# A hand-ordered attention and MoE kernel: one chunk's convolution moves from TensorE to VectorE, and the written order of all work is replaced

## The chip, the cores and the metric

The kernel runs on one core of a Trainium2 chip. The metric is the device time of one execution in microseconds (us). Three runs of the kernel before gave 212.16, 212.40 and 213.29 us, median 212.4.

## The reference

Two stages follow each other. The first is a gated linear attention with a running state of 48x48 for each of 4 batches and 8 heads over 768 steps. The second takes its output x (768 steps of 384 channels for each batch), makes a gate by a causal convolution over 5 steps, and multiplies the gate with a projection:

```python
f = 1 / (1 + exp(-f_logit))
for t in range(768):
    state = f[t][:, None] * state + outer(k[t], v[t])
    y[t] = q[t] @ state
x = y, heads side by side                      # 4 x 768 x 384
gate_pre[t] = sum(conv_w[j] * x[t - 4 + j] for j in range(5))   # channel by channel
out = (sigmoid(gate_pre) * (x @ w_val)) @ w_out
```

Everything is float32. The weights of the second stage come as int64 pairs (float64 bits) and are turned into float32 on the chip.

## The kernel before

**Chunks and units.** The 768 steps are cut into 6 chunks of 128 (C = 128, chunk c). A pair of heads lies on 112 of the 128 partitions, and BP = 16 is 4 batches x 4 pairs. The second stage goes in 8 units: chunk 0 is units 0 and 1 (two batches each), chunks 1 to 4 are units 2 to 5 (four batches each), chunk 5 is units 6 and 7 (two batches each).

**Attention in a chunk.** ScalarE makes exp and ln of the gate logits (`pexp`, `pln`, tile `e`), VectorE sums the logarithms along the steps (`scan`), ScalarE makes the two exponentials (`exp2`, `exp1`), VectorE multiplies them into k and q (`pmulk`, `pmulq`, tiles `kb`, `qb`). For each batch b, TensorE then makes the scores of 8 heads (`scores`, into the one PSUM tile `aps`), VectorE masks them while it copies them to SBUF (`mask`, tile `asb`), and TensorE applies them to v and adds q times the old state (`apply`, into a PSUM bank `bk`). ScalarE copies the result into `xf` (`xevac`). In parallel TensorE transposes k (`ktrans`), ScalarE copies it (`kevac`, tile `ksb`), TensorE makes the state's increment (`dstate`), and VectorE adds and decays it (`stadd`, `stmul`); a DMA (`stcopy`) puts the new state in place.

**Second stage of a unit.** `msplit` (ScalarE) and `mlow` (VectorE) split x into two parts, `mval` is its projection on TensorE (9 matmuls for each of 3 column blocks m), `mmul` (VectorE) multiplies it by the gate, `mhigh` (ScalarE) and `mrest` (VectorE) split the product, `mout` (TensorE, 9 matmuls) projects it out, and `mstore` (ScalarE) copies it to one of two buffers `osb`, from which a DMA stores it. The gate itself has two forms. Either TensorE convolves (`conv n j`, five taps j, 12 matmuls of 32x32 blocks each, every float32 matmul two instructions in the trace; tile `wd` holds the taps), and `gate` (ScalarE) takes the sigmoid from PSUM. Or ScalarE makes the last tap (`mlast n m`) and VectorE adds the other four, one `SCALAR_TENSOR_TENSOR` each (`mtap n m j`, gt <- xf, cws, gt), before `gate`. Before, units 0 to 3 (chunks 0 to 2) use TensorE, units 4 to 7 VectorE. The constant CS = 3 is the first chunk whose channels are laid out for the second form: `place`, `wturn` and `halo` turn by it, and in chunk CS the 4 steps of the chunk before (`halo`) come by DMAs (tile `xf`), in other chunks by a VectorE copy.

**What sets the order.** Nothing is scheduled by a tool: the string PROGRAM lists every piece of work, and `Ordered` chains each engine's instructions (TensorE, VectorE, ScalarE, and SyncE, which issues all DMAs) in just that order. An engine takes its list one by one; a piece that waits for another engine holds up all behind it on its own engine. Between engines there are only data dependencies: `aps` is one tile, so the next `scores` waits for the `mask` before it, and the six banks `bk` are handed round.

`busy n` puts n bfloat16 matmuls on a tile of zeros (tile `idle`) on TensorE; their result is not used.

```python
def busy(n):
    for _ in range(n):
        PE.matmul(free[-1][:], idle[:, 0:128], idle[:], start=True, stop=True)
```

All the operations are emitted through one helper line, so that the profile names them all L119 and tells them apart by their tiles. The kernel ends with a check of ranges (`okc`, `sums`, `cnt`), on whose result a general path, not taken here, would run.

Of the kernel before, what the change touches and what calls it, by code (L numbers as in the profile page):

```python
# [32 lines left out]
CS = 3  # L33
# [11 lines left out]
halo 0; loadf 0 0; loadf 0 1; loadv 0 1; wload 0; loadk 0 1; loadv 0 2; loadv 0 0; loadq 0 0; loadq 0 1; pexp 0 0;  # L45
loadk 0 0; loadk 0 2; loadq 0 2; loadf 1 0; pln 0 0; pexp 0 1; wload 1; scan 0 0; weight 0; wload 2; pln 0 1;
loadk 1 0; exp2 0 0; scan 0 1; exp1 0 0; loadv 1 0; pexp 0 2; loadf 2 0; pmulq 0 0; exp2 0 1; loadq 1 0; exp1 0 1;
pmulk 0 1; pln 0 2; pmulk 0 0; busy 24; ktrans 0 1; pmulq 0 1; ktrans 0 0; kevac 0 1; scores 0 0; scan 0 2;
kevac 0 0; weight 0; dstate 0 0; dstate 0 1; weight 0; exp2 0 2; weight 0; weight 0; mask 0 0; exp1 0 2;
pmulk 0 2; busy 4; scores 0 1; pexp 1 0; apply 0 0; loadk 2 0; pmulq 0 2; ktrans 0 3; okc 0; xevac 0 0; ktrans 0 2;  # L50
mask 0 1; weight 1; pln 1 0; scores 0 3; stadd 0 0; weight 0; stcopy 0 0; taps; weight 2; kevac 0 2; apply 0 1;
kevac 0 3; scan 1 0; weight 2; dstate 0 3; loadv 2 0; dstate 0 2; xevac 0 1; loadq 2 0; weight 1; conv 0 0;
conv 0 1; msplit 0; weight 2; conv 0 2; exp2 1 0; weight 2; conv 0 3; weight 2; conv 0 4; exp1 1 0; mask 0 3;
gate 0 1; scores 0 2; pmulk 1 0; apply 0 3; stadd 0 1; gate 0 2; loadk 2 1; gate 0 0; mask 0 2; loadf 3 0;
ktrans 1 0; xevac 0 3; ktrans 1 1; kevac 1 0; weight 2; apply 0 2; kevac 1 1; scan 1 1; weight 2; dstate 1 1;
loadv 2 1; dstate 1 0; xevac 0 2; weight 2; msplit 1; conv 1 0; loadq 2 1; conv 1 1; weight 4; pexp 2 0;
stadd 1 0; conv 1 2; stcopy 0 1; pmulq 1 0; conv 1 3; conv 1 4; weight 1; scores 1 1; weight 1; weight 1;
exp2 1 1; mask 1 1; gate 1 2; pmulk 1 1; scores 1 0; gate 1 1; apply 1 1; loadk 3 0; mask 1 0; exp1 1 1; halo 1;
ktrans 1 3; weight 1; ktrans 1 2; mlow 0; apply 1 0; xevac 1 1; kevac 1 2; pmulq 1 1; weight 1; dstate 1 2;
kevac 1 3; weight 1; wturn 0; stmul 1 0; scores 1 2; xevac 1 0; okc 1; pln 2 0; mlow 1; weight 3; mval 0 0;  # L60
stcopy 1 0; mask 1 2; mval 1 1; loadv 3 0; weight 3; loadq 3 0; scan 2 0; wturn 1; weight 4; apply 1 2; pexp 3 0;
mval 1 2; mmul 1 1; weight 3; xevac 1 2; mval 0 2; weight 3; exp2 2 0; weight 3; dstate 1 3; exp1 2 0;
mmul 1 2; scores 1 3; mmul 0 2; weight 3; pln 3 0; mval 0 1; loadk 3 1; mask 1 3; mval 1 0; pmulq 2 0; weight 3;
apply 1 3; gate 1 0; weight 3; mmul 0 1; weight 4; weight 4; xevac 1 3; loadv 3 1; loadq 3 1; weight 4;
msplit 2; conv 2 0; halo 2; weight 4; conv 2 1; mmul 0 0; weight 4; conv 2 2; mmul 1 0; weight 4; pmulk 2 0;
conv 2 3; mhigh 0 0; mlow 2; scores 2 1; mhigh 1 2; mhigh 0 2; mhigh 0 1; ktrans 2 0; mhigh 1 1; conv 2 4; mrest 0 2;
kevac 2 0; mrest 0 0; mhigh 1 0; mrest 0 1; dstate 2 0; mrest 1 1; mout 0 1; mrest 1 2; gate 2 1; mrest 1 0;
gate 2 2; mout 0 2; mask 2 1; gate 2 0; mstore 0 1; mval 2 1; stadd 1 1; mstore 0 2; stmul 1 1; scan 2 1; loadf 4 0;
stcopy 1 1; scores 2 0; mout 0 0; mmul 2 1; exp2 2 1; mask 2 0; mout 1 0; mout 1 2; scan 3 1; mstore 0 0; mstore 1 0;
apply 2 0; exp1 2 1; pexp 4 0; pmulk 2 1; apply 2 1; okc 2; pmulq 2 1; ktrans 2 3; loadq 4 0; xevac 2 0; ktrans 2 2;  # L70
xevac 2 1; scan 3 0; ktrans 2 1; scores 2 2; kevac 2 2; loadk 4 0; kevac 2 1; kevac 2 3; dstate 2 2; dstate 2 1;
exp2 3 1; dstate 2 3; mask 2 2; loadv 4 0; mval 2 2; exp1 3 1; stadd 2 1; mstore 1 2; pmulq 3 1; pln 4 0; scores 2 3;
mmul 2 2; apply 2 2; pmulk 3 1; loadk 4 1; exp2 3 0; stadd 2 0; exp1 3 0; ktrans 3 3; stmul 2 0; ktrans 3 2;
pmulk 3 0; xevac 2 2; stcopy 2 0; mout 1 1; kevac 3 2; kevac 3 3; dstate 3 2; pmulq 3 0; mstore 1 1; ktrans 3 1;
ktrans 3 0; mhigh 2 1; dstate 3 3; mask 2 3; kevac 3 1; mval 2 0; kevac 3 0; mhigh 2 2; mrest 2 1; mrest 2 2;
scores 3 1; mmul 2 0; dstate 3 1; okc 3; mhigh 2 0; stmul 2 1; dstate 3 0; mrest 2 0; apply 2 3; loadf 5 0;
stadd 3 0; stmul 3 0; mout 2 0; scan 4 1; xevac 2 3; loadq 4 1; loadv 4 1; msplit 3; halo 3; conv 3 0; mstore 2 0;
mlow 3; stcopy 2 1; exp2 4 1; conv 3 1; exp1 4 1; conv 3 2; mask 3 1; conv 3 3; pexp 5 0; pmulk 4 1; scores 3 0;
pmulq 4 1; conv 3 4; pln 5 0; loadk 5 0; mask 3 0; apply 3 1; stadd 3 1; gate 3 0; stmul 3 1; apply 3 0; scan 5 0;
xevac 3 1; scores 3 2; gate 3 2; loadv 5 0; stcopy 3 0; xevac 3 0; ktrans 4 2; scan 5 1; gate 3 1; mval 3 0;  # L80
loadq 5 0; kevac 4 2; mask 3 2; exp2 5 1; dstate 4 2; mval 3 2; mmul 3 0; scan 4 0; exp1 5 1; scores 3 3; apply 3 2;
loadk 5 1; mmul 3 2; exp2 4 0; mask 3 3; mout 2 2; exp1 4 0; pmulk 4 0; xevac 3 2; okc 4; exp2 5 0; apply 3 3;
pmulq 4 0; mstore 2 2; pmulk 5 1; exp1 5 0; scores 4 0; stcopy 3 1; pmulk 5 0; xevac 3 3; ktrans 4 0; mout 2 1;
loadv 5 1; kevac 4 0; loadq 5 1; pmulq 5 0; mask 4 0; mval 3 1; mhigh 3 2; mhigh 3 0; mrest 3 2; mstore 2 1;
mrest 3 0; apply 4 0; mlast 4 2; mmul 3 1; mlast 4 0; mtap 4 2 0; mhigh 3 1; scores 4 1; mtap 4 0 0; xevac 4 0;
mrest 3 1; msplit 4; ktrans 4 1; mask 4 1; mout 3 1; kevac 4 1; mtap 4 0 1; mlast 4 1; mtap 4 0 2; dstate 4 1;
mstore 3 1; mout 3 0; mtap 4 2 1; mtap 4 2 2; mlow 4; scores 4 3; mstore 3 0; apply 4 1; halo 4; mtap 4 1 0;
mtap 4 1 1; ktrans 4 3; xevac 4 1; mask 4 3; mval 4 1; kevac 4 3; mtap 4 1 2; mtap 4 2 3; apply 4 3; okc 5; gate 4 2;
pmulq 5 1; scores 4 2; mtap 4 1 3; xevac 4 3; mtap 4 0 3; dstate 4 3; gate 4 1; dstate 4 0; mask 4 2; mout 3 2;
gate 4 0; stadd 4 0; mmul 4 1; apply 4 2; mstore 3 2; stmul 4 0; stadd 4 1; mhigh 4 1; stcopy 4 0; stmul 4 1;  # L90
scores 5 1; xevac 4 2; mrest 4 1; stcopy 4 1; halo 5; mlast 5 1; mval 4 0; mask 5 1; mtap 5 1 0; scores 5 0;
mtap 5 1 1; mmul 4 0; apply 5 1; mask 5 0; mhigh 4 0; mrest 4 0; apply 5 0; xevac 5 1; mtap 5 1 2; mlast 5 0;
# [38 lines left out]
def gla_moe(ctx: ExitStack, tc: tile.TileContext, q, k, f, v, wv, cw, wo, out):  # L131
# [165 lines left out]
    slot = lambda c, b: (B * c + b) % 2  # L297
    place = lambda c, m, z: (z + TURN[m]) % 4 if c >= CS else z

# [419 lines left out]
```

## Time and profile before

| what | before |
|---|---|
| median of 3 runs | 212.4 us |
| the profiled execution | 211.6 us, of which its span is 209.9 us |
| TensorE matmuls busy | 190.1 us |
| TensorE weight loads busy | 151.8 us |
| VectorE busy | 171.5 us |
| ScalarE busy | 133.3 us |
| GpSimd busy | 17.9 us |
| mean granted TensorE clock | 0.98 |

The profile shows one execution. Its engines are PE (TensorE matmuls), PEld (TensorE weight loads), DVE (VectorE), ACT (ScalarE), POOL (GpSimd) and SP (SyncE). Busy time is the union of an engine's instructions. A row of groups gives the engine, the operation, output <- input, the number of instructions, their busy time in us, the mean of one in ns, and the idle time just ahead of them with what ended it. A row of windows gives from:to, the length, the busy time of each engine with its instructions, the granted clock, the DMA engines' share and GB/s. A row of waits reads: who waited, for whom, us in total, times, the longest. A row of the timeline or of the chain begins with the start in us and the length.

### The profile page before, as it was taken

The numbers are of one execution on the slowest core, as the hardware profiler recorded it, in microseconds if no ns is written. First come the engines' busy times: TensorE is split into PE (matmuls) and PEld (weight loads), VectorE is DVE, ScalarE is ACT, GpSimd is POOL, SyncE is SP. The second block draws the span as 40 slices with busy tenths as digits, with TensorE's granted clock in tenths as the row PEclk, the third lists the DMA queues.
The fourth block names the chain that finished last, engine by engine and source line by source line (L and its number), as shares of the span: only waits on it lengthen the run. The fifth ranks groups of instructions, "written<-read, shape, count | busy, mean of one in ns | idle before, by whom it ended". The sixth has DMA issues, their size and how long they took to land.

```text
span 209.9 us, 6753 instructions
## 1 busy us (share of the span) xinstructions
PE 190.1 (91%) x2974; PEld 151.8 (72%) x2974; DVE 171.5 (82%) x233; ACT 133.3 (63%) x205; POOL 17.9 (9%) x19
## 2 busy tenths in 40 slices
PE   0988959869998989999999999999999999999970
PEld 0356748658995579988857788788888888798970
DVE  6469987867989989899799999698979999797700
ACT  3677974976995665796299866663642843744630
POOL 4000200603120910000000000000000000000000
PEclk9999997979999999999999999999999999999998
DMA  5899999963595037464395633702022001200431
GB/s 181 262 419 430 411 418 334 403 210 100 127 292 203 31 80 250 141 204 130 119 292 164 170 123 105 242 2 104 3 65 46 3 0 50 103 0 3 150 125 41
DMA packets 20372, 34.28 MB, mean 163 GB/s; under 512 B 10992, under 2 KB 13296, under 8 KB 19184
## 3 DMA queue, kind: packets, MB, share of 16 engines
q1 hardware_dynamic: 20336, 33.78, 47.7%
q8 instruction: 25, 0.41, 0.9%
q14 instruction: 11, 0.09, 0.1%
HBM read 26.77 MB, written 4.72 MB: 150 GB/s over the span
## 4 chain that ended last, share of the span: by engine, by line
PE 73%; DVE 10%; DMA 5%; issue 3%; POOL 3%; SPq 2%; ACT 1%; ACTq 0%; DVEq 0%
PE bk L119 61%; PE aps L119 11%; DMA qb<-in_q 3%; POOL woL L254 3%; DVE e L119 2%; DVE qb L119 2%; DVE asb L119 2%; SPq L119 2%; DMA out<-osb 2%; DVE cb L119 1%; DVE ca L119 1%; DVE kb L119 1%; ACT osb L119 1%; ACT woH L119 0%; DVE ss L119 0%
## 5 line engine op out<-in xcount | busy, mean ns | idle before, releaser
L119 ACT ACTIVATE e<-e 112x1024 f32<-112x1024 f32 (+2 forms) x42 | 48.7, 1177 | 7.5 <-DMA e<-in_f 4.1
L119 DVE TENSOR_TENSOR asb<-aps,tri 128x1024 f32<-128x1024 f32 x24 | 29.4, 1223 | 10.0 <-PE aps L119 9.0
L119 PE MATMUL bk<-asb,vb 128*32 128x128 f32 x768 | 36.1, 283 | 0.0
L119 PE MATMUL aps<-qb,kb 48*128 48x128 f32 x384 | 29.7, 292 | 5.8 <-DVE asb L119 3.9
L119 PEld LDWEIGHTS aps<-qb,kb 48*128 48x128 f32 x384 | 24.5, 192 | 13.6 <-issue 5.5
L119 PEld LDWEIGHTS bk<-asb,vb 128*32 128x32 f32 x768 | 31.3, 114 | 0.8 <-issue 0.2
L119 PE MATMUL bk<-qb,st 112*32 112x128 f32 x480 | 30.6, 281 | 0.0
L119 PE MATMUL bk<-rg,woH 128*128 128x512 f32 (+1 forms) x108 | 29.9, 363 | 0.0
L119 DVE TENSOR_TENSOR_SCAN e<-keep,e 112x1024 f32<-112x1024 bf16 (+1 forms) x13 | 27.5, 2119 | 2.8 <-ACT e L119 2.8
L119 ACT COPY osb<-bk 128x256 f32<-128x256 f32 (+1 forms) x24 | 11.5, 479 | 21.7 <-PE bk L119 14.6
L119 PEld LDWEIGHTS bk<-qb,st 112*32 112x32 f32 x480 | 21.8, 112 | 4.4 <-issue 2.6
L119 ACT COPY xf<-bk 128x384 f32<-128x384 f32 x24 | 11.5, 478 | 17.8 <-PE bk L119 17.7
L119 PEld LDWEIGHTS bk<-rg,woH 128*128 128x128 f32 x108 | 18.4, 188 | 3.0 <-issue 0.4
L119 PE MATMUL bk<-rg,woL 128*128 128x512 f32 (+1 forms) x54 | 19.3, 357 | 0.9 <-POOL woL L254 0.9
L119 DVE SCALAR_TENSOR_TENSOR gt<-xf,cws,gt 128x512 f32<-128x512 f32 x24 | 17.5, 747 | 0.3
L119 DVE TENSOR_TENSOR qb<-qb,e 112x1024 f32<-112x1024 f32 (+1 forms) x13 | 16.1, 1236 | 1.9 <-DMA qb<-in_q 1.9
L119 PE MATMUL bk<-xf,wd 32*32 32x256 f32 (+1 forms) x480 | 16.4, 487 | 0.9 <-ACT xf L119 0.6
L119 PE MATMUL bk<-xH,wvH 128*128 128x512 f32 (+1 forms) x42 | 15.6, 372 | 0.0
L119 ACT CAST rg<-gt 128x512 fp32r<-128x512 f32 (+1 forms) x18 | 9.4, 547 | 8.9 <-DVE gt L119 7.1
L119 DVE TENSOR_TENSOR kb<-kb,e 112x1024 f32<-112x1024 f32 (+1 forms) x13 | 14.7, 1138 | 0.2 <-DMA kb<-in_k 0.2
L119 PE MATMUL bk<-xL,wvH 128*128 128x512 f32 (+1 forms) x42 | 14.5, 344 | 0.0
L119 PE MATMUL bk<-xH,wvL 128*128 128x512 f32 (+1 forms) x42 | 14.5, 344 | 0.0
(90 smaller groups left out, 313.1 us busy)
## 6 DMA issues: line engine op xcount, KB each, us to landing
e<-in_f SPq DMA_DIRECT2D x5, 1024.0 KB, 8.8
kb<-in_k SPq DMA_DIRECT2D x9, 512.0 KB, 4.5
qb<-in_q SPq DMA_DIRECT2D x9, 512.0 KB, 5.5
vb<-in_v SPq DMA_DIRECT2D x9, 448.0 KB, 5.1
out<-osb SPq DMA_DIRECT2D x12, 256.0 KB, 2.0
out<-osb SPq DMA_DIRECT2D x12, 128.0 KB, 1.7
st<-ss SPq DMA_DIRECT2D x20, 72.0 KB, 2.6
raww<-in_wv SPq DMA_DIRECT2D x1, 1152.0 KB, 10.4
```

The lines of the kernel that those rows point to most:

```text
L119: ins = emit(*a, **kw)
L254: nc.gpsimd.tensor_tensor(out=dst[1], in0=x, in1=dst[0].bitcast(F32), op=ALU.subtract)
```

## The change

CS goes from 3 to 2. In PROGRAM the five `conv 3 j` are gone (unit 3 is chunk 2), and three `mlast 3 m` and twelve `mtap 3 m j` are there instead. The whole string is written in a new order. The fillers were `busy 24` and `busy 4` and are `busy 20`, `busy 3`, `busy 2` and `busy 5`. No function is changed.

```diff
-CS = 3
+CS = 2
...
-pmulk 0 1; pln 0 2; pmulk 0 0; busy 24; ktrans 0 1; pmulq 0 1; ktrans 0 0; kevac 0 1; scores 0 0; scan 0 2;
...
+scan 0 1; loadv 1 0; exp2 0 0; loadq 1 0; exp1 0 0; pmulk 0 0; pln 0 2; pmulq 0 0; busy 20; ktrans 0 0; scores 0 0;
...
```

The order at three places, as the built kernels have it. The number behind a tile's name is its address slot, so `asb_83` and `asb_84` are the two buffers of masked scores; x4 behind a row counts equal instructions that follow one another; L119 is L120 in the changed kernel.

VectorE, at the start of the real work, before (two scans of chunk 0, then q, k, k, q of its first two pieces, the third scan, the first mask):

```order
L119 SCALAR_TENSOR_TENSOR e_79<-keep,e_79 112x512 x2
L119 TENSOR_TENSOR qb_64<-qb_64,e_79 112x512
L119 TENSOR_TENSOR kb_66<-kb_66,e_82 112x512 x2
L119 TENSOR_TENSOR qb_64<-qb_64,e_79 112x512
L119 SCALAR_TENSOR_TENSOR e_79<-keep,e_79 112x1024
```

VectorE at the same place now:

```order
L120 SCALAR_TENSOR_TENSOR e_79<-keep,e_79 112x512 x2
L120 TENSOR_TENSOR kb_66<-kb_66,e_82 112x512
L120 TENSOR_TENSOR qb_64<-qb_64,e_79 112x512
L120 SCALAR_TENSOR_TENSOR e_79<-keep,e_79 112x1024
L120 TENSOR_TENSOR qb_64<-qb_64,e_79 112x512
L120 TENSOR_TENSOR kb_66<-kb_66,e_82 112x512
```

The first piece's k and q stand first now, and the large scan comes between the two pieces. In the queue of loads, which SyncE issues, the first pieces of k and q have moved ahead of those of v and of the small weight `cw`.

TensorE in chunk 0, before (two transposes, the third scores, an apply, two state increments, and the first convolution matmul of unit 0):

```order
L119 MATMUL bk_111<-ident,kb_66 128x112 x4
L119 MATMUL bk_112<-ident,kb_66 128x112 x4
L119 MATMUL aps<-qb_64,kb_66 128x128 x8
L119 MATMUL bk_107<-asb_84,vb_68 32x128 x16
L119 MATMUL bk_108<-vb_68,ksb_88 48x48 x8
L119 MATMUL bk_108<-vb_68,ksb_87 48x48 x8
L119 MATMUL bk_110<-xf_91,wd 32x256
```

TensorE at the same place now:

```order
L120 MATMUL bk_111<-ident,kb_66 128x112 x4
L120 MATMUL bk_112<-ident,kb_66 128x112 x4
L120 MATMUL aps<-qb_64,kb_66 128x128 x8
L120 MATMUL bk_107<-vb_68,ksb_88 48x48 x8
L120 MATMUL bk_109<-asb_84,vb_68 32x128 x16
L120 MATMUL bk_107<-vb_68,ksb_87 48x48 x8
L120 LDWEIGHTS idle
L120 MATMUL bk_109<-idle 128x512
```

An increment stands ahead of the apply, and fillers stand where the convolution of unit 0 stood; that convolution comes after the fourth scores and their apply.

VectorE around the first mask of chunk 3, before (a state product, the next scan, the low part of unit 3's x, the mask, k and q of chunk 4, the next mask):

```order
L119 TENSOR_TENSOR ss<-u_89,e_79 112x384
L119 SCALAR_TENSOR_TENSOR e_80<-keep,e_80 112x1024
L119 TENSOR_TENSOR xL<-xf_91,xH 128x1536
L119 TENSOR_TENSOR asb_84<-aps,tri 128x1024
L119 TENSOR_TENSOR kb_66<-kb_66,e_82 112x1024
L119 TENSOR_TENSOR qb_64<-qb_64,e_80 112x1024
L119 TENSOR_TENSOR asb_83<-aps,tri 128x1024
```

VectorE there now, from the first mask of chunk 3 on:

```order
L120 TENSOR_TENSOR asb_84<-aps,tri 128x1024
L120 SCALAR_TENSOR_TENSOR gt<-xf_91,cws,gt 128x512 x4
L120 TENSOR_TENSOR u_90<-ss,bk_110 112x384
L120 TENSOR_TENSOR gt<-bk_107,gt 128x512
L120 TENSOR_TENSOR asb_83<-aps,tri 128x1024
L120 TENSOR_TENSOR xL<-xf_91,xH 128x1536
L120 TENSOR_TENSOR rg_907<-gt,rg_906 128x512
L120 SCALAR_TENSOR_TENSOR gt<-xf_91,cws,gt 128x512 x3
L120 TENSOR_TENSOR asb_83<-aps,tri 128x1024
```

The twelve taps of unit 3 stand here in runs of four, three and five between the masks (the five lie some rows further down, and hold the last tap of one block and the four of the next).

More of the change, by code (lines that the diff above doesn't have):

```diff
@@ L50 @@
[L50 to L89, printed above, removed]
@@ L106 @@
+mstore 6 0; mrest 7 2; gate 7 1; mmul 7 1; mhigh 7 1; mout 5 2; mstore 5 0; mrest 7 1; mout 7 1; mstore 5 2;
+mout 7 2; mstore 7 1; mout 7 0; mstore 7 2; mout 6 2; mstore 7 0; mstore 6 2
 """
```

79 lines of the change are left out of this document (59 added, 20 removed).

## The prediction

> **What bounds the kernel now.** I began with the page: the span, the engines' busy time, and its slices.
>
> ```profile
> span 209.9 us, 6753 instructions
> PE 190.1 (91%) x2974; PEld 151.8 (72%) x2974; DVE 171.5 (82%) x233; ACT 133.3 (63%) x205; POOL 17.9 (9%) x19
> PE   0988959869998989999999999999999999999970
> DVE  6469987867989989899799999698979999797700
> PEclk9999997979999999999999999999999999999998
> ```
>
> TensorE is near full from the second slice on, and without a hole over the last two thirds. VectorE is next, at nine tenths for most of the way. The averages hide where the kernel still has room, so I cut the span: the front (up to chunk 2's first scores, about 69 us), the body up to the last VectorE work, and the tail. The columns are from:to, length, then busy time of PE, PEld, DVE, ACT and POOL, the clock, DMA share and GB/s.
>
> ```profile
> 12.00:69.00 57.00, 49.67 (x1039) 39.25 (x1037) 49.56 (x62) 44.97 (x62) 10.11 (x8) 0.94 0.82 299
> 69.00:199.00 130.00, 129.06 (x1886) 105.76 (x1881) 115.41 (x157) 79.31 (x127) 5.12 (x1) 1.00 0.34 103
> 199.00:210.00 11.00, 4.36 (x39) 4.12 (x37) 0.45 (x3) 2.08 (x5) 0.00 (x0) 0.92 0.26 85
> ```
>
> In the body TensorE is idle for 0.94 us of 130: there it alone sets the pace, and a microsecond taken off it is a microsecond gained, as long as VectorE keeps up. VectorE is idle there for 14.6 us, and for 7.4 in the front, 22.0 in all. In the front neither is full. The waits say what VectorE's idle time is and what stops TensorE:
>
> ```profile
> DVE asb L119 <- PE aps L119: 9.0, 13, 1.9
> DVE rg L119 <- ACT rg L119: 3.8, 4, 1.6
> PE aps L119 <- DVE asb L119: 3.9, 4, 1.3
> PE bk L119 <- POOL woL L254: 0.9, 1, 0.9
> ```
>
> VectorE waits most for scores to mask: it comes early, since TensorE is behind. TensorE's own waits are in the front, but for the one for GpSimd at 74 us.
>
> Last, the end, from VectorE's timeline (first row) and the chain of waits:
>
> ```profile
> 198.26 0.43 DVE L119 TENSOR_TENSOR rqb<-re,rkb 128x256 fp32r<-128x256 f32 x1 [0.16 <-ACT rkb L119]
> ...
> 199.04 0.60 ACT osb L119
> 199.65 2.00 DMA out<-osb
> 201.65 0.02 issue
> ```
>
> VectorE's last product for the output ends at 198.7; from there to the span's end are 11.2 us of last projections, copies and stores that wait for one of two buffers.
>
> **The change part by part.** *TensorE loses the convolution of chunk 2.* The first row is the convolution's own busy time (tile wd) around its place, the second the price of one tap on VectorE, the third and fourth what ScalarE pays.
>
> ```profile
> 105.00:113.00 8.00, 5.20 (x120) 2.04 (x120) 0.00 (x0) 1.00 0.80 232
> ```
>
> ```profile
> L119 DVE SCALAR_TENSOR_TENSOR gt<-xf,cws,gt 128x512 f32<-128x512 f32 x24 | 17.5, 747 | 0.3
> L119 ACT ACTIVATE gt<-xf,cws 128x512 f32<-128x512 f32 x6 | 4.2, 724 | 3.0 <-DVE rg L119 2.9
> L119 ACT ACT_TABLE_LOAD x10 | 12.8, 1283 | 1.0 <-PEq L710 0.8
> xf<-xf SPq DMA_DIRECT2D x1, 8.0 KB, 6.0
> ```
>
> TensorE is 5.2 us shorter. VectorE gets 12 taps; 24 of them take 17.5 us together, so 12 take 8.8. ScalarE gets three last taps, 3 x 0.72 = 2.2 us, and by the new order two more table loads, 2 x 1.28 = 2.6; it is idle for 51 us of the body, so I take nothing for them (if that cover were gone, at most 4.8). The halo of chunk 2 now comes by DMA in place of chunk 3's; its longest piece shown took 6.0 us to land. It is issued once chunk 1's output is copied, and its first reader, a tap behind chunk 3's first mask, stands a whole chunk of TensorE work later: nothing, with 6.0 as the bound if it were late. The columns turned by CS cost no instruction more.
>
> *The front.* VectorE's first product waits for q, and TensorE's first work for that product:
>
> ```profile
> 4.54 0.63 ACT L119 ACTIVATE e<-e 112x512 f32<-112x512 f32 x1 [2.44 <-DMA e<-in_f]
> 7.63 0.63 ACT L119 ACTIVATE e<-e 112x512 f32<-112x512 f32 x1 [1.70 <-DMA e<-in_f]
> 8.38 2.76 ACT L119 ACTIVATE e<-e 112x512 f32<-112x512 f32 x4
> ...
> ```
>
> ```profile
> 12.17 0.69 DVE L119 TENSOR_TENSOR qb<-qb,e 112x512 f32<-112x512 f32 x1 [1.90 <-DMA qb<-in_q]
> ```
>
> The new queue puts the first k and q directly behind the gate logits, so that wait goes. What is late next is ScalarE: by the new list, behind the ln that begins at 8.38 (0.6), comes a large exp (1.1 by the page's mean of 1058 ns for that size, below, with its 0.2 of accumulator), then the first exponential (0.6), so the first product starts at about 10.8 instead of 12.2. I take 1.4 us; the bounds are nothing (if k's load, now the third transfer in the queue, is later than that) and 1.9, the wait itself.
>
> ```profile
> L119 ACT ACTIVATE e<-e 112x1024 f32<-112x1024 f32 x24 | 25.4, 1058 | 3.2 <-DVE e L119 2.7 <-DVE kb L119 0.2
> ```
>
> *The fillers.* The front has a second loss, the clock, seen in steps of 2 us:
>
> ```profile
> 30.00:32.00 2.00, 1.05 (x9) 0.93 (x8) 0.61 (x2) 0.45 (x2) 0.00 (x0) 0.70 1.02 424
> 32.00:34.00 2.00, 2.00 (x35) 1.41 (x33) 1.77 (x2) 0.00 (x0) 0.00 (x0) 0.50 1.04 363
> 44.00:46.00 2.00, 1.73 (x18) 1.49 (x22) 0.19 (x1) 1.99 (x2) 0.00 (x0) 0.62 0.54 157
> 46.00:48.00 2.00, 2.00 (x48) 1.85 (x44) 2.00 (x4) 0.09 (x1) 0.00 (x0) 0.53 0.53 160
> ```
>
> After holes of about 1 us between scores the granted clock fell to 0.50 and 0.53. In these four rows the matmuls lost 1.05 x 0.30 + 2.00 x 0.50 + 1.73 x 0.38 + 2.00 x 0.47 = 2.9 us. The new fillers stand just in such holes of chunk 0, and in chunk 1 four transposes now stand between the first two scores. TensorE can get 2.9 us back and the holes besides; if the fillers sit ahead of ready work instead, ten of them cost about 3 us:
>
> ```profile
> L119 PE MATMUL bk<-idle 128*128 128x512 bf16 x28 | 9.0, 490 | 5.0 <-DVE bk L119 5.0
> ```
>
> (9.0 / 28 = 0.32 each.) Neither end moves the sum below as long as VectorE is the later engine, which the next step shows.
>
> *Who sets the end now.* TensorE from its start to its end is busy 49.67 + 129.06 + 4.36 = 183.1 us; without the convolution 177.9, and 175.0 with the clock back. Without holes from 12 us on it would be through at 187 to 190 us; now it is at 199 + 4.36 = 203.4. VectorE has 49.56 + 115.41 = 165.0 us of work after 12 us, and 173.8 with the taps. From 10.8 to 198.7 are 187.9, so 14.1 us remain to spread: all that VectorE may still wait, where it waited 22.0, if the end is not to move. So VectorE becomes the engine that sets the end, and the size of the gain is how much of its idle time goes.
>
> *How much of it goes.* Two things bear on it. First the order: I added up both lists with start-to-start prices as in these rows (a mask 1.13, a product 1.13):
>
> ```profile
> 107.94 1.22 DVE L119 TENSOR_TENSOR asb<-aps,tri 128x1024 f32<-128x1024 f32 x1
> 109.07 1.22 DVE L119 TENSOR_TENSOR kb<-kb,e 112x1024 f32<-112x1024 f32 x1
> 110.20 1.22 DVE L119 TENSOR_TENSOR qb<-qb,e 112x1024 f32<-112x1024 f32 x1
> ```
>
> In the old list, the work written ahead of chunk 2's first scores comes to 51.5 us on both engines, and ahead of the very last scores to 146.5 on TensorE and 136.2 on VectorE: as written, VectorE falls 10 us behind in work, and that is idle time. In the new list the two sums are 51.0 and 51.5, then 147.6 and 147.3, and never over 1.2 us apart between them. The new order asks both engines to be full at once. Second, what VectorE reaches when it is fed:
>
> ```profile
> 110.00:120.00 10.00, 10.00 (x212) 7.63 (x198) 9.54 (x9) 9.15 (x12) 0.00 (x0) 1.00 0.64 166
> 120.00:130.00 10.00, 10.00 (x164) 8.07 (x162) 9.45 (x10) 7.07 (x9) 0.00 (x0) 1.00 0.36 122
> ```
>
> Over these 20 us, with both engines full, it is at 95%. I take 95% throughout: 173.8 / 0.95 = 182.9, of which 9.1 are idle. From 10.8 that ends at 193.7, 5.0 us before the 198.7 of now. With the same 11.2 us behind it (the new list ends in four small projections, the old in three with a large store; within 1 us either way), the span is 204.9.
>
> *The sum.* The profiled execution took 211.6, 1.7 over its span; 204.9 + 1.7 = 206.6. The median of the runs is 0.8 above the profiled one, so I predict 207.4 against 212.4.
>
> **The rivals.** All go by one number, VectorE's idle time between its first product and its last: each microsecond of it over 9.1 adds one to 207.4.
>
> *VectorE does not pack* (slower). Its list is in order, and so is TensorE's: a mask that comes late holds the next scores, those the next mask, and an engine without slack never makes up a hole. If it keeps its 22.0 us, the end comes at 10.8 + 173.8 + 22.0 = 206.6, 7.9 later than now: 220.3. It decides from 14.1 us of idle time (no change) and by over 0.5% from 15.2 on; the place is the body, where all twelve taps lie. For it speak the 9.0 us of waits for scores, that VectorE rarely held 95% for more than 20 us, and chains over ScalarE (tap, sigmoid, product, split) that the sums of two engines do not see. Against it, most of those waits were VectorE being early. The Trainium skill's rule in Perfetto Trace Analysis, section Identifying the Most-Contended Engine, takes this side: it judges TensorE by its weight loads, not by its matmuls, so here VectorE (82%) and not TensorE (72%) would be the most contended, and the change adds to it. By that rule the whole 8.8 us of taps would come on top, 221.2. The body's row with TensorE at 129.06 of 130 speaks against it.
>
> *TensorE stays the bound*. If VectorE gets by with under 6 us of idle time, it is through by 190.6 and the span 201.8 or less: 204.3 and below, with TensorE's holes in the front left as its own limit. For it: the two lists are in step, and the machine repeats its times within 0.5%, so an order fitted to measured times may hold. Against it: chunk 0 alone is a chain of ScalarE, VectorE and TensorE in turn, and 7.4 us were lost in the front.
>
> *No change*: idle time between 13.0 and 15.2, the gain of TensorE and the load of VectorE cancelling out.
>
> **How the numbers follow.** About 0.5%, 1.06 us, is what a measurement of this kernel can tell from no change, so faster means below 211.3, slower above 213.5. Idle time from 6 to 13.0 us, my forecast (204.3 to 211.3): 0.48. Under 6: 0.25. Both are faster, 0.73. No change 0.10. Slower, over 15.2: 0.17, with the weight on the first few microseconds. For the range I leave out what needs under 3.7 us of idle time, less than 2% of VectorE's work (202.0), and what keeps over 15.7 (214.0). That takes in the front's bounds of +1.4 and -0.5 us, too.
>
> **What would show it.** In the profile after, VectorE's busy time should be 180 us (171.5 + 8.8) and its share of the body 95%; TensorE's 5 us lower but for fillers; the group of taps 36 of 128x512. TensorE should now wait for VectorE in the body in pieces of some tenths of a microsecond. The first k product should start near 10.8 and the clock stay above 0.9 between 28 and 47 us. The forecast is wrong if VectorE's idle time between its first and last product is over 13 us (then look for what it waits for: scores, or ScalarE's splits), or if it is under 6 and TensorE still has no hole. If VectorE is full and the end is late all the same, the price of a tap was wrong, or one of the last stores.

## The result and the profile after

| | before | after |
|---|---|---|
| median (runs) | 212.73 us (4) | 207.28 us (4: 204.25 to 208.32) |
| profiled execution | 211.6 us | 204.25 us |
| its span | 209.9 us | 202.5 us |

The ratio is 0.966, with a 95% interval of 0.955 to 0.977: faster. All medians here are of all runs, while the ratios and their intervals compare only the fast runs, which lie within 1.5% of the fastest of their kernel (here 204.25 and 206.75 us); by the medians the ratio is 0.974. The profiled execution is the fastest of the four. What sets it apart from the other three is the clock, and comes up under the second group of experiments.

The page of the kernel after: span, busy time, and three of its rows of 40 slices.

```profile
span 202.5 us, 6522 instructions
PE 181.2 (89%) x2856; PEld 148.8 (73%) x2856; DVE 179.7 (89%) x245; ACT 136.2 (67%) x210; POOL 13.9 (7%) x19
PE   0998895896977999999999999999999999999950
DVE  7689999399999999998999999999999999999500
PEclk9999999999999999999999999999999999999996
```

TensorE has lost 8.9 us and VectorE gained 8.2, and by the totals both are at 89%. The slices say more. VectorE, which ran at eight and nine tenths, now has one gap (the eighth slice, 35 to 41 us) and nines after it. TensorE is without a hole from the fourteenth slice on (before, from the sixteenth). By stages, cut at VectorE's last product (columns from:to, length, PE, PEld, DVE, ACT, POOL, clock, DMA share, GB/s):

```profile
12.00:69.00 57.00, 48.15 (x1074) 37.68 (x1073) 52.36 (x62) 42.25 (x61) 11.44 (x9) 1.00 0.89 315
69.00:190.37 121.37, 121.37 (x1728) 104.06 (x1727) 118.14 (x165) 84.21 (x132) 0.00 (x0) 1.00 0.32 98
190.37:202.50 12.13, 4.68 (x40) 4.40 (x38) 0.72 (x5) 2.09 (x6) 0.00 (x0) 0.84 0.28 93
```

In the body TensorE is busy 121.37 us of 121.37, and VectorE 118.14, which is 97%. TensorE's work from 12 us on is 48.15 + 121.37 + 4.68 = 174.2 us, where it was 183.1. All of its 8.85 us of idle time (57.00 - 48.15) lies in the front.

The chain of waits that ended last (start, length, what) comes into TensorE at 65 us and stays there to the tail:

```profile
by line: PE bk L120 53.2%; PE aps L120 8.6%; DMA out<-osb 1.8%; DVE e L120 1.1%; ACT osb L120 0.7%; DVE qb L120 0.6%; DVE xL L120 0.4%; DVE gt L120 0.2%; issue 0.1%; ACTq L120 0.0%
...
65.11 0.34 DVE gt L120
65.45 0.04 issue
65.50 1.33 PE bk L120 x9
```

The waits, first VectorE's longest for TensorE, then three of TensorE's (total, times, longest):

```profile
DVE asb L120 <- PE aps L120: 3.8, 3, 3.3
```

```profile
PE bk L120 <- issue: 4.7, 2, 3.0
...
PE bk L120 <- DVE gt L120: 1.1, 1, 1.1
PE aps L120 <- DVE asb L120: 0.5, 1, 0.5
```

VectorE's 13 waits for scores (9.0 us) are three (3.8 us), nearly all of it in one of 3.3 us. TensorE's wait for GpSimd's weights is gone from the list. What has grown is "issue", time in which TensorE waited for nothing that the profile shows: 4.7 us in two pieces, 3.0 and 1.7. Before has 2.8 us of it, in four pieces of at most 1.2.

### The profile page after: what moved, and what is told of

Read it like the earlier page. It is cut to its first block, busy times and chain, and to the rows that moved or that the text cites. A ratio compares the mean times of both kernels' runs of the same rounds, so it can differ in the third digit from the quotient of the medians.

```text
span 202.5 us, 6522 instructions
## 1 busy us (share of the span) xinstructions
PE 181.2 (89%) x2856; PEld 148.8 (73%) x2856; DVE 179.7 (89%) x245; ACT 136.2 (67%) x210; POOL 13.9 (7%) x19
## 4 chain that ended last, share of the span: by engine, by line
PE 62%; DVE 2%; DMA 2%; ACT 1%; issue 0%; ACTq 0%
PE bk L120 53%; PE aps L120 9%; DMA out<-osb 2%; DVE e L120 1%; ACT osb L120 1%; DVE qb L120 1%; DVE xL L120 0%; DVE gt L120 0%; ACTq L120 0%
## 5 line engine op out<-in xcount | busy, mean ns | idle before, releaser
L120 ACT ACTIVATE e<-e 112x1024 f32<-112x1024 f32 (+2 forms) x42 | 48.9, 1179 | 6.9 <-DVE e L120 3.5
L120 PE MATMUL bk<-asb,vb 128*32 128x128 f32 x768 | 35.2, 273 | 2.2 <-issue 1.7
L120 DVE TENSOR_TENSOR asb<-aps,tri 128x1024 f32<-128x1024 f32 x24 | 29.2, 1217 | 3.8 <-PE aps L120 3.8
L120 PEld LDWEIGHTS bk<-asb,vb 128*32 128x32 f32 x768 | 30.1, 109 | 1.9 <-DVE asb L120 1.0
L120 PE MATMUL bk<-qb,st 112*32 112x128 f32 x480 | 30.0, 275 | 0.0
L120 PE MATMUL bk<-rg,woH 128*128 128x512 f32 (+1 forms) x108 | 29.5, 361 | 0.0
L120 DVE TENSOR_TENSOR_SCAN e<-keep,e 112x1024 f32<-112x1024 bf16 (+1 forms) x13 | 27.6, 2121 | 1.7 <-ACT e L120 1.7
L120 PE MATMUL aps<-qb,kb 48*128 48x128 f32 x384 | 27.9, 285 | 0.5 <-DVE asb L120 0.5
L120 PEld LDWEIGHTS aps<-qb,kb 48*128 48x128 f32 x384 | 23.3, 187 | 5.5 <-issue 2.5
L120 DVE SCALAR_TENSOR_TENSOR gt<-xf,cws,gt 128x512 f32<-128x512 f32 x36 | 26.7, 749 | 0.6
L120 PEld LDWEIGHTS bk<-qb,st 112*32 112x32 f32 x480 | 21.3, 109 | 4.1 <-issue 2.7
L120 ACT COPY osb<-bk 128x256 f32<-128x256 f32 (+1 forms) x24 | 11.3, 476 | 15.7 <-PE bk L120 11.8
L120 PEld LDWEIGHTS bk<-rg,woH 128*128 128x128 f32 x108 | 18.6, 188 | 3.1
L120 PE MATMUL bk<-rg,woL 128*128 128x512 f32 (+1 forms) x54 | 19.2, 356 | 0.0
L120 ACT COPY xf<-bk 128x384 f32<-128x384 f32 x24 | 11.4, 474 | 9.0 <-PE bk L120 9.0
L120 DVE TENSOR_TENSOR qb<-qb,e 112x1024 f32<-112x1024 f32 (+1 forms) x13 | 16.0, 1231 | 0.6 <-ACT e L120 0.6
L120 PE MATMUL bk<-idle 128*128 128x512 bf16 x30 | 10.0, 496 | 5.9 <-DVE bk L120 5.0
L120 DVE TENSOR_TENSOR kb<-kb,e 112x1024 f32<-112x1024 f32 (+1 forms) x13 | 14.7, 1136 | 0.3 <-ACT e L120 0.3
L120 PE MATMUL bk<-xH,wvH 128*128 128x256 f32 (+1 forms) x36 | 13.2, 367 | 1.1 <-DVE gt L120 1.1
L120 PE MATMUL bk<-xf,wd 32*32 32x256 f32 (+1 forms) x360 | 10.5, 450 | 3.9 <-issue 3.0
L120 PE MATMUL bk<-xL,wvH 128*128 128x256 f32 (+1 forms) x36 | 12.1, 337 | 0.0
```

Of the source, the lines that this page charges most:

```text
L120: ins = emit(*a, **kw)
```

## The experiments

All times are medians; the kernel before was run beside each set: 212.92 us with e1 to e4, 212.74 with e5 to e8, 211.16 with e9 to e12; the three sets ran on three chips. The diffs of PROGRAM list only the pieces that change.

### Is it the moved work or the order?

**e1_taps_old_order**: the kernel before with chunk 2's convolution on VectorE, everything else where it was.

```diff
-CS = 3
+CS = 2
-conv 3 0; conv 3 1; conv 3 2; conv 3 3; conv 3 4
+mlast 3 0; mlast 3 2; mlast 3 1; mtap 3 0 0 ... mtap 3 1 3     (in the places of the conv pieces and behind masks)
```

> The move alone: the order of before, in which only unit 3's convolution gives way to 3 last taps on ScalarE and 12 taps on VectorE. Theory (the order pays, the move alone does not): TensorE loses 5.2 us of work, but VectorE gets 8.8 us in a stretch of about 25 us in which it was 95% busy, so the masks of chunk 3 come late and TensorE waits 3 to 8 us for them: 209 to 215 us against 212.7. Rival (the move pays by itself): TensorE has no new wait and the time falls by the convolution's 5.2 us, to 207.5.

Measured: 220.44 us (218.15 to 222.67), ratio 1.044 (1.034 to 1.054). By the medians 7.5 us slower. The windows where the taps stand, then the waits:

```profile
100.00:120.00 20.00, 15.36 (x254) 12.82 (x250) 19.36 (x23) 13.53 (x17) 0.00 (x0) 0.83 0.60 185
120.00:140.00 20.00, 15.96 (x197) 12.91 (x198) 18.11 (x18) 11.63 (x16) 0.00 (x0) 0.91 0.34 104
```

```profile
PE bk L117 <- ACT ksb L117: 4.5, 1, 4.5
PE aps L117 <- DVE asb L117: 4.2, 1, 4.2
```

VectorE is busy for 37.5 us of these 40 and TensorE is idle for 8.7. It waits 4.2 us for a mask that stands behind two taps and other VectorE work, and 4.5 us for ScalarE's copy of transposed k (`ksb`), which stands behind a sigmoid that itself waited 5.3 us for taps. Its clock falls to 0.83 and 0.91. This is the first rival of the prediction, VectorE does not pack, with the chain over ScalarE that it names, but in the old order. VectorE's idle time between its first and last product is 18.0 us in the profiled execution (218.15 us), where the rival had 22.0 for its 220.3; that the median is so near to that time is chance.

**e2_conv_new_order** and **e8_conv_new_order**: the new order with chunk 2's convolution left on TensorE. In e2 unit 3's sigmoid of block 0 stands ahead of unit 2's product with that block, which so takes the wrong gate; e8 has the sigmoid behind it.

```diff
-CS = 2
+CS = 3
-mlast 3 0..2; mtap 3 0..2 0..3
+conv 3 0; conv 3 1; conv 3 2; conv 3 3; conv 3 4; gate 3 2; gate 3 1     (behind mval 2 0)
+gate 3 0     (e2: with the other gates; e8: behind mrest 2 0)
```

> The order alone: the new order with unit 3's convolution back on TensorE, its five taps where the first four VectorE taps and the first sigmoid stood. VectorE has 8.8 us less, TensorE 5.2 us more. Theory (both engines are full in the new order, and from 65 us on TensorE sets the end): 5 us slower than the new kernel, 210 to 213 us. Rival of the prediction (VectorE alone sets the end): no slower than the new kernel, 207 us or less.

> The order alone once more, as in e2, with the sigmoid of unit 3's first block put behind the last use of unit 2's gate, which e2 had overwritten. Theory (both engines are full in the new order): 5 us above the new kernel run beside it. Rival (VectorE alone sets the end): not slower than it.

Measured: e2 212.87 us, ratio 1.000 (0.995 to 1.005); e8 212.94 us (209.68 to 213.62). The kernel after, run again beside e8 as e6, takes 207.87 (206.71 to 208.49). So TensorE's 5.2 us of convolution come on top with 5.1 us, and VectorE's 8.8 us less buy nothing. Executions at a like clock say the same: 209.68 us (clock 0.995) against 204.25 (0.991), and 212.84 to 213.62 (0.965 to 0.971) against 206.71 to 208.49 (0.967 to 0.977). The body of e8, with the cut of before, and VectorE's waits in it:

```profile
69.00:199.00 130.00, 129.27 (x1878) 108.59 (x1879) 113.95 (x158) 86.24 (x135) 0.00 (x0) 1.00 0.31 95
```

```profile
DVE u L116 <- PE bk L116: 6.2, 2, 5.8
DVE asb L116 <- PE aps L116: 5.8, 5, 2.5
```

TensorE is full, VectorE waits for it. The four corners (old and new order, convolution there or here) are 212.9, 220.4, 212.9 and 207.3 to 207.9: the move alone costs 7.5 us, the order alone brings nothing by the medians, both together bring 5. (Single executions at a clock of 0.995 or 0.996, 209.25 and 209.68 us with the order alone against 210.74 and 210.95 before, leave room for about 1 us of the order's own.) The old order was tried with one placement of the twelve taps, so it is not shown that no other would do, nor which part of the new order makes room for them.

### What are the 3 us of "issue", and why do runs differ?

**e6_new_again**: the kernel after, unchanged.

> The new kernel unchanged, for its spread on the same chip as the other runs here. Theory (a hole of 3 us brings the clock down in some runs and not in others): runs of about 204 with a mean clock near 0.99 and runs of 206 to 208 with a clock near 0.97, and nothing in between that the clock does not explain. Rival: the spread has nothing to do with the clock.

Measured: 207.87 us, ratio 0.977 (0.972 to 0.982). Its profiled execution is one of 207.4 us, and shows what the first profile did not. None of its six runs is near 204 us, and their mean clocks are 0.967 to 0.977. First both executions' timeline of TensorE in unit 0's and unit 1's convolution (in brackets the idle time before), after and then e6:

```profile
29.17 3.85 PE L120 MATMUL bk<-xf,wd 32*32 32x256 f32 x173 [0.34 <-DVE wd L120]
36.03 1.75 PE L120 MATMUL bk<-xf,wd 32*32 32x256 f32 x67 [3.02 <-issue]
```

```profile
29.68 3.85 PE L120 MATMUL bk<-xf,wd 32*32 32x256 f32 x173 [0.61 <-DVE wd L120]
37.02 1.93 PE L120 MATMUL bk<-xf,wd 32*32 32x256 f32 x67 [3.49 <-issue]
```

Both stop behind the 173rd matmul for 3.0 and 3.5 us. The windows behind it, after (one row), then e6:

```profile
40.00:44.00 4.00, 4.00 (x94) 3.31 (x94) 3.97 (x6) 2.87 (x7) 2.28 (x2) 1.00 1.05 362
```

```profile
36.00:40.00 4.00, 2.98 (x77) 2.19 (x79) 0.10 (x1) 1.08 (x4) 0.00 (x0) 0.81 1.01 395
40.00:44.00 4.00, 4.00 (x26) 3.56 (x24) 2.96 (x4) 1.57 (x4) 0.00 (x0) 0.50 0.98 349
```

In e6 the granted clock is 0.50 for the whole second window. There 16 transposes took 3.25 us; the same 16 take 1.75 at full clock (e9's timeline, below, has them so):

```profile
40.89 3.25 PE L120 MATMUL bk<-ident,kb 112*128 112x112 f32 x16
```

VectorE's wait for scores there is 4.9 us instead of 3.3, and its whole idle time between first and last product 11.8 us (184.66 - 172.87) instead of 8.1. That is the 3 us between the profiled 204.25 and a usual run. The Trainium skill, TensorE: Matmul & The Clock Gate, section Why this matters for your kernels, puts the limit for a drop of the clock at gaps of about 3 us. These two executions, one on each side, agree; e5 below (0.58 behind a hole of 2.44 us) and the kernel before do not: its row of 32 to 34 us with 0.50, shown in the prediction, lies behind a hole of 1.21 us and this one:

```profile
30.95 1.23 PE L119 MATMUL aps<-qb,kb 48*128 48x128 f32 x9 [1.18 <-issue]
```

The traces also keep every change of the granted clock with its time, and these show what decides. In each of the fourteen traces all changes lie whole multiples of 3.41 us apart, on a grid that stands elsewhere in every execution. Of the windows of this grid that ran at full clock, every one in which TensorE was idle for 1.91 us or more was followed by a clock of 0.50, and none with 1.82 us or less was. Here are the two windows that hold the hole, for after and then for e6 (the first busy time is TensorE's):

```profile
31.39:34.81 3.42, 1.63 (x76) 1.09 (x57) 3.42 (x5) 3.40 (x4) 0.00 (x0) 1.00 1.05 335
34.81:38.22 3.41, 2.19 (x75) 1.59 (x77) 0.79 (x3) 0.98 (x4) 0.00 (x0) 1.00 1.05 376
```

```profile
31.63:35.04 3.41, 1.90 (x92) 1.37 (x71) 3.41 (x4) 3.39 (x4) 0.00 (x0) 1.00 1.06 318
35.04:38.45 3.41, 1.43 (x67) 1.07 (x67) 1.06 (x3) 0.54 (x2) 0.00 (x0) 1.00 1.04 388
```

In after the grid splits the hole so that TensorE is idle for 1.79 and 1.22 us; in e6 for 1.51 and 1.98, and the clock falls at 38.45. In before one window holds nearly all of its two holes, 2.26 us. This is read from the traces; no run shifted the grid on purpose.

**e3_no_fillers**: the fillers `busy 3; busy 2; busy 5` out. **e4_loads_late**: four loads moved behind the burst. **e7_loads_after_state**: six loads moved behind a state copy, near 55 us. Each asks whether fillers or loads make the hole.

```diff
 e3: -busy 3 -busy 2 -busy 5
 e4: -loadk 2 0 -loadv 2 0 -loadq 2 0 -loadf 3 0          +the same four behind conv 1 4
 e7: -loadk 2 0/1 -loadv 2 0/1 -loadq 2 0/1               +the same six behind stcopy 1 0
```

> The new kernel without the three groups of fillers inside chunk 0 (3, 2 and 5; the 20 ahead of the first work stay). Theory (they keep the clock): the granted clock falls to about 0.5 for 2 to 4 us somewhere in 15 to 34 us, and the work there comes 1 to 2 us later; since VectorE is full from there on, the end comes 1 to 2 us later. Rival (they fill time in which nothing is late): no difference within 0.5 us, the clock at 1.00.

> The new kernel with four loads (the first halves of chunk 2's k, v and q, and chunk 3's gate logits; 2.5 MB) issued some 6 to 10 us later, behind the convolution of unit 1. Theory (TensorE's holes of 3.0 and 1.7 us without a visible wait are its instruction stream, fetched in blocks over DMA engines that the loads keep full): the hole at 33 us shrinks to under 1 us, VectorE's wait of 3.3 us behind it with it, and the time falls by 2 to 3 us, to about 205. Rival (the hole has nothing to do with the loads): it stays at 3 us and the time does not move, or rises if the loads now come late.

> The new kernel with the six loads of chunk 2's k, q and v (3 MB) issued behind the state copy of chunk 1, which SyncE can only issue near 47 us, so that the DMA engines run dry between about 32 and 47 us. Theory (the instruction blocks are late because they queue behind loads): the hole at 33 us shrinks to under 1.5 us, and the one at 46 us too; 204 to 206 us if the loads still come in time for the products near 62 to 70 us. Rival (a block takes that long whatever the DMA engines do): the hole stays at 3 us and the time at 205 to 208 or above.

Measured: e3 208.37 us, ratio 0.981 (0.974 to 0.989); e4 208.30 us, 0.981 (0.974 to 0.989); e7 217.3 us, 1.013 (1.006 to 1.020). The holes are 3.40, 3.49 and 3.60 us, still there. Without the fillers the clock in 12 to 24 us is 0.72 instead of 1.00, but the time is within 1.1 us of the kernel after, in ranges that overlap, so what the fillers are worth is not clear. In e4 and e7 the DMA share in 32 to 36 us is 1.06 and 1.07 all the same, since older loads are under way until 36 us and later; so neither took the traffic away from the hole, and the hole itself does not tell whether traffic makes it. e7 then waits for chunk 2's late k (`PE bk <- ACT ksb` 6.8 us), which is its price.

What they do tell is where the hole lies. Here are windows that start at zero and end within the hole (in before within its 0.33 us hole at 37.6), for before and e3:

```profile
0.00:37.60 37.60, 28.16 (x474) 18.51 (x475) 29.01 (x42) 26.09 (x42) 5.42 (x14) 0.95 0.93 350
```

```profile
0.00:38.20 38.20, 25.36 (x474) 18.65 (x475) 31.50 (x45) 29.26 (x41) 4.12 (x13) 0.91 0.95 362
```

The second count is the weight loads: 475 in both, and 475 in after, e4, e5, e6 and e7 too, whatever work they belong to (a few matmul records are missing). In e3, with ten filler matmuls gone ahead of it, the hole comes about ten matmuls later in the burst, with 58 recorded ones left behind it instead of 67:

```profile
38.46 2.40 PE L117 MATMUL bk<-xf,wd 32*32 32x256 f32 x58 [3.40 <-issue]
```

The next hole of the kernel after (1.7 us) comes behind 730 of them: 255 pairs of weight load and matmul later, 510 instructions.

**e5_fill_in_burst**: twelve wide fillers (`warm 12`: 128x512, into the bank `aps`, free there) behind the seventh of the ten taps.

```diff
 conv 0 4;
+warm 12;
 pmulk 1 0
...
+def warm(n):
+    for _ in range(n):
+        PE.matmul(aps[:, 0].rearrange("t p n -> t (p n)"), idle[:, 0:128], idle[:], start=True, stop=True)
```

> The new kernel with 12 fillers (bfloat16, on the free scores tile) between the seventh and the eighth of the ten taps of the two convolutions of chunk 0, some 29 matmuls ahead of the hole of 3.0 us. Theory (the hole is the next block of 256 instructions being late: 128 pairs of weight load and matmul are through in 3 us there, and a block takes longer to come): the 2.6 us of fillers come out of the hole, which falls to about 0.5 us, nothing is lost, and since TensorE is never idle for 3 us the granted clock stays at 1.00 behind it in every run: 204 to 205 us in all runs, against 204 to 208 for the new kernel. Rival (the hole is a fixed stall of these matmuls, or of a dependency): it stays 3 us and the fillers come on top, 2 us slower.

Measured: 207.34 us (205.5 to 208.32), ratio 0.973 (0.968 to 0.979). TensorE's timeline:

```profile
33.52 1.03 PE L117 MATMUL aps<-idle 128*128 128x512 bf16 x4 [0.16 <-issue]
36.98 3.17 PE L117 MATMUL aps<-idle 128*128 128x512 bf16 x7 [2.44 <-issue]
```

Behind it the clock fell, for a shorter time than in e6:

```profile
36.00:40.00 4.00, 3.02 (x7) 0.89 (x7) 0.09 (x1) 0.00 (x0) 0.00 (x0) 0.58 1.03 398
```

The expected 0.5 us did not come, and the rival's fixed place did not hold either. The hole has moved into the fillers, behind the fifth (of which four are recorded), which wait for nothing: 168 + 5 = 173 matmuls into the burst again. So it is no property of the convolution, of a buffer or of data: it stands at a count of instructions. The fillers stood too late for a cure, five instead of some thirty pairs ahead of it.

**e9_fill_earlier**: the same twelve fillers behind the fifth tap, 120 pairs into the burst.

```diff
 conv 0 3;
+warm 12;
 pmulq 1 0
```

> The changed kernel with 12 wide fillers (128x512, bf16, of the zero tile, into a bank that is free there) behind the fifth of the ten convolution taps, 120 matmul pairs into the burst. Theory: the hole of 3 us before matmul 729 is the wait for the next 128 matmul pairs of the instruction stream; twelve wide matmuls take 12 x 0.22 = 2.6 us of TensorE time but only 12 pairs, and here they are done ahead of the boundary, so the stream catches up while TensorE works. The hole shrinks from 3.0 to 3.5 us to 0.5 us or less, the clock of 36 to 48 us stays at 1.00 in every run, and every run takes 204 to 205 us, where the changed kernel took 204.25 to 208.5. Rival 1, the hole comes from the convolution's own work or from a buffer: it stays at 3 us and the fillers come on top, 209 to 211 us. Rival 2, the clock of 36 to 48 us falls for another reason than the hole: the hole is gone, the clock still falls to 0.50 there, 207 to 208 us.

(The 3-us hole is the one behind matmul 475; 729, as the expectation says, is the place of the second one.) Measured: 204.97 us (204.33 to 205.35), ratio 0.968 (0.963 to 0.974). The timeline:

```profile
29.49 2.79 PE L117 MATMUL bk<-xf,wd 32*32 32x256 f32 x120 [0.61 <-DVE wd L117]
32.44 2.54 PE L117 MATMUL aps<-idle 128*128 128x512 bf16 x11 [0.16 <-issue]
34.91 1.29 PE L117 MATMUL bk<-xf,wd 32*32 32x256 f32 x41
36.57 2.00 PE L117 MATMUL bk<-xf,wd 32*32 32x256 f32 x79 [0.37 <-issue]
...
39.60 1.75 PE L117 MATMUL bk<-ident,kb 112*128 112x112 f32 x16
```

The burst resumes at 36.57, when it always did, but the hole is 0.37 us and TensorE has been busy meanwhile. In this execution the clock stays at 1.00. Six runs lie within 1.0 us, with mean clocks of 0.98 to 0.994; the ten runs of the kernel after lie between 204.25 and 208.49, with clocks of 0.966 to 0.991. By the ratios to before, e9 is 0.9% better than e6, but the intervals touch and the two were not run side by side; what is plain is that the runs of 206 us and more are gone, in e9's six as in the eight of e11 and e12 that build on it.

**e10_burst_in_quiet**: e9 with 384 very small matmuls at 70 us.

```diff
+burst 384;
 mval 1 0
...
+PE.matmul(free[-1][0:32, 0:32], idle[:, 0:32], idle[:, 0:32], start=True, stop=True)     (n times)
```

> The kernel of e9 with 384 very small matmuls (32x32, bf16, of the zero tile, into a free bank) ahead of the value projection of unit 1, near 70 us, where the DMA engines are nearly empty (share 0.03 to 0.05): three blocks of 128 pairs, each far faster than the 2.9 us of 128 convolution pairs. It asks whether a block of instructions takes 6 us because the DMA engines are full of loads, or always. If it is the loads: no hole over 0.5 us in the burst, which then takes 384 pairs x 0.023 to 0.03 us = 9 to 12 us. If a block always takes as long as at 30 to 36 us, some 5 to 6 us from one boundary to the next: two or three holes of 2 to 4 us each, and the burst takes 16 to 20 us. Between the two: holes of about 1 us. The total time, one look, follows: 213 to 216 or 220 to 225 us.

Measured: 215.15 us, one run. The page's row on the fetch of instructions, of e9 and then of e10 (packets, MB, share), and TensorE's timeline of the burst:

```profile
q8 instruction: 24, 0.39, 0.8%
```

```profile
q8 instruction: 27, 0.44, 0.9%
```

```profile
69.84 6.94 PE L117 MATMUL bk<-idle 128*32 128x32 bf16 x271
76.97 2.99 PE L117 MATMUL bk<-idle 128*32 128x32 bf16 x113 [0.19 <-issue]
```

384 pairs are 768 instructions, and cost 3 packets more: 256 instructions in a packet of 16 KB (0.39 MB / 24). And in the quiet the stream keeps up, three packets in 10.1 us with 0.19 us of hole, 3.4 us for 128 pairs (10.12 / 3). At 30 to 37 us, with the DMA share at 1.0 and over, about 6 us pass from one boundary to the next: in e9 the boundary before the one at 36.57 is 128 pairs back, some 46 into the burst, at about 30.6. So the hole is TensorE waiting for its next 128 pairs, which come late where loads fill the DMA engines. The traces also keep when each q8 packet moved. At 475, in all fourteen of them (DMA share 0.98 to 1.06), the packet starts 3.3 to 4.4 us after TensorE began the 128 pairs ahead of that place, moves in 1.1 to 1.5 us, and TensorE goes on 1.2 to 1.6 us after that. In e7 the loads are gone when the next block begins (DMA share 0.22 in 36 to 40 us), and that packet starts after 1.2 us, where it took 3.5 to 4.2 in the other thirteen. So what the loads lengthen is mainly the packet's wait for its start; its transfer took 0.9 us in e7 and 1.0 to 1.2 in the others. That the hole at 475 itself would go without them was not tested; taking the loads away from the burst was tried (e4, e7) and didn't come off.

### Which engine sets the end?

**e11_vector_light** leaves out five of unit 3's taps, 3.7 us of VectorE's work; **e12_tensor_light** leaves out the low part of the weights in the value projections of units 3 and 4, 4.1 us of TensorE's. Both go by e9, on the same chip.

```diff
 e11: -mtap 3 1 3 -mtap 3 0 0 -mtap 3 0 1 -mtap 3 0 2 -mtap 3 0 3
 e12: -for w, a in ((wH, aH), (wH, aL), (wL, aH)):
      +for w, a in ((wH, aH), (wH, aL), (wL, aH))[:terms]:        (terms = 2 for units 3 and 4)
```

> The kernel of e9 without five of VectorE's taps in the middle of the body (the last tap of block 1 and four taps of block 0 of unit 3): part of unit 3's convolution is left out. VectorE has 5 x 0.75 = 3.7 us less to do, TensorE the same. If TensorE sets the end, as its full row of 69 to 190 us says: 0 to 0.8 us less than e9. If VectorE sets the end, as the prediction had it: 3.0 to 3.7 us less. If both are full and each waits for the other in turn: between, some 1.5 to 2.5 us less.

> The kernel of e9 where the value projections of units 3 and 4 leave out the third of their three terms (the low part of the weights): part of the product's accuracy is left out. TensorE has 18 matmuls of 128x512 less, 18 x 0.228 = 4.1 us, VectorE the same. If TensorE sets the end: 2.5 to 4.1 us less than e9, the upper end if VectorE has that much slack. If VectorE sets the end: 0 to 0.8 us less.

Measured, beside e9's 204.97: e11 205.06 us (203.99 to 205.72), e12 203.65 us (203.01 to 204.86). VectorE's 3.7 us are worth nothing. TensorE's 4.1 us are worth 1.3, though the runs of e12 and e9 overlap, so this size is not firm. The windows of 69 to 190 us, e11 first, and e12's chain by engine:

```profile
69.00:190.00 121.00, 121.00 (x1727) 103.89 (x1727) 114.95 (x159) 84.20 (x133) 0.00 (x0) 1.00 0.33 98
```

```profile
69.00:190.00 121.00, 118.77 (x1718) 101.28 (x1717) 118.71 (x164) 84.27 (x135) 0.00 (x0) 1.00 0.32 98
```

```profile
DVE 33%; PE 25%; issue 4%; ACT 3%; DMA 2%; ACTq 0%; DVEq 0%
```

With less VectorE work TensorE is still full and VectorE just waits more. With less TensorE work most of the chain goes over to VectorE, which was then about 1.3 us behind. Neither the "TensorE alone" price (2.5 to 4.1) nor the "VectorE alone" one (0 to 0.8) held for e12: TensorE sets the end (e8 and e11), and VectorE is next, by about a microsecond if e12's size holds.

## Why the prediction came out, step by step

It said 207.4, and the median is 207.28. For the profiled execution it said 206.6, which took 204.25. Both halves of that belong in the account.

**TensorE's work: right.** 175.0 us of it from 12 us on were forecast, with the clock back; 174.2 are there.

**VectorE's work: right.** Twelve taps more, at the old price:

```profile
L120 DVE SCALAR_TENSOR_TENSOR gt<-xf,cws,gt 128x512 f32<-128x512 f32 x36 | 26.7, 749 | 0.6
```

That is 9.2 us more than before for 8.8 forecast; VectorE in all is at 179.7 for 180. ScalarE grew by 2.9 us, and no wait for a halo shows among VectorE's: hidden, as taken.

**The front: mis-sized.** It was to bring 1.4 us, at most 1.9, and brought 2.8. ScalarE's, then VectorE's timeline:

```profile
6.36 0.63 ACT L120 ACTIVATE e<-e 112x512 f32<-112x512 f32 x1 [0.38 <-DMA e<-in_f]
```

```profile
9.34 0.69 DVE L120 TENSOR_TENSOR kb<-kb,e 112x512 f32<-112x512 f32 x1 [0.34 <-ACT e L120]
```

The bound counted the wait for q alone. But the second load of the gate logits, which stands second in the queue in both kernels, is there at 6.36 instead of 7.63, and all of chunk 0 begins 1.3 us sooner. What comes behind it in the queue has changed; which of it made the load sooner was not tried.

**VectorE's idle time: right in size.** 9.1 us were taken. Between its first and last product:

```profile
9.34:190.37 181.03, 172.18 (x2809) 142.73 (x2808) 172.91 (x228) 128.56 (x195) 11.44 (x9) 1.00 0.51 171
```

181.03 - 172.91 = 8.1, in a usual run (e6) 11.8. Both lie in the forecast case (6 to 13).

**The tail: 0.9 us too short.** 12.1 us from VectorE's last product to the end, for 11.2; TensorE still has 4.68 us of matmuls there (4.36 before), and the last copies wait for stores out of two buffers.

The sum against the profile: first product 1.5 sooner, work 0.9 less (172.9 for 173.8), idle time 1.0 less, tail 0.9 more; in all 2.4 us less, 202.5 for 204.9.

**Who sets the end now: wrong.** The step "VectorE becomes the engine that sets the end" failed. It compared TensorE without holes, 187 to 190 us, with VectorE at 95%. TensorE kept its holes in the front (8.85 us, for 7.33 before), and has none behind, so its last matmul comes at 12 + 174.2 + 8.85 = 195.05 us; VectorE ran at 97% in the body, not 95%. The sign that the prediction named, TensorE waiting for VectorE in the body in pieces of some tenths of a microsecond, did not appear: TensorE has no idle time there. e8 and e11 show that TensorE is first, and e12 puts VectorE about 1.3 us behind. That the sum by VectorE came near all the same is since the two are that close, and since the 95% was read from two windows of before in which both engines were full. Of VectorE's 8.1 us of idle time, 3.8 are now waits for TensorE's scores; the rest is mostly short waits for ScalarE. The mechanism of the rival *TensorE stays the bound* held, though its condition, under 6 us of idle time on VectorE, did not.

By that error the fillers and the clock were given no term "as long as VectorE is the later engine". They have one. **The step from the profile to the median: mis-sized**, 3.0 us instead of 0.8. In e6's profiled execution, and by their mean clocks in most others, the hole brings the clock down, TensorE is late with its scores, and the whole body with it. The prediction saw two stretches of lowered clock in before and gave them to holes between scores; it left the 2.8 us of "issue" out of TensorE's waits, and didn't see that three of these holes fall at a count of instructions (1.18, 0.33 and 0.74 us behind 348, 475 and 602 weight loads), and that new wide work in one place does nothing for a burst of 173 small matmuls in another. "The clock above 0.9 between 28 and 47 us" came true in the profiled execution and not in the usual one. So that the median came within 0.1 us is luck: two errors, of 2.4 and 2.2 us, cancel.

**The rivals.** VectorE does not pack: refuted in the new order, and what happens without it (e1). The rule of the Trainium skill that it leaned on (Perfetto Trace Analysis, section Identifying the Most-Contended Engine, by which VectorE and not TensorE was most contended before) does not hold here: with the order held fixed, 5.2 us on TensorE cost 5.1 (e8 against e6), and 3.7 us on VectorE nothing (e11). No change: what the new order alone gives (e2, e8).

## What to carry to other kernels

Where two engines that work from written lists are both near full, moving work and reordering are one change: summing both lists up to each point where they meet (here the scores) told beforehand that the new lists are in step, and windows of 20 us in which VectorE was already 95% busy told, in e1's expectation, that the old order had no room there. A row that shows an engine busy for all of a stage is a better judge of what sets the end than shares of the whole span, and the test is cheap: take a few microseconds off each engine in turn, as e11 and e12 do. And the "issue" wait that stayed at the same count of instructions when the work around it was changed was the instruction stream; a few wide matmuls ahead of the boundary gave it time to catch up.

## What the runs showed of the hardware

TensorE's instructions arrive in packets of 16 KB, 256 instructions (e10: three packets for 768). A burst of 128 pairs of weight load and small matmul takes 2.9 us, and with the DMA engines full TensorE could begin the next 128 only about 6 us after these: a hole of 3.0 to 3.6 us at weight load 475, in the seven traces whose burst of small matmuls lay ahead of it without wide ones (before, with other work ahead of it there, had 0.33). The Trainium skill, Runtime: NRT & Kernel Launch, section Instruction fetch mechanics, has the blocks of 256 instructions and calls the cost of their boundaries mostly hidden. The count agrees with the rows of e9 and e10. The cost was hidden at 70 us (0.19 us) and not at 33 us.

The hole costs more than its length. Behind it the clock went to 0.50 in six of the eight traces with a hole of over 2 us there, for 3.4 to 10.2 us, and not at all in the other two; between after, where it did not, and e6, where it did, are 3 us at the end of the kernel. The length of the hole does not decide: one of 3.02 us and one of 3.22 (e2) left the clock at 1.00, ones of 2.44 and 3.49 us did not. What decides, in all fourteen traces, is how the idle time falls on the grid of 3.41 us: 1.91 us and more in one window brought the clock down, 1.82 us and less did not. In e9, with 0.37 us of hole left, TensorE was idle for no more than 1.5 us in any window at full clock before the tail.
